# Attention products on block-diagonal matrices, or as 64x64 tiles of TensorE

## The chip, the cores and the metric

The kernel runs on one core of one Trainium2 chip. The core has five engines with an instruction queue each: TensorE (PE) for matmuls, VectorE (DVE), ScalarE (ACT) and GpSimd (POOL) for elementwise work, and SyncE (SP), which here issues nearly all DMAs. PE's weight loads have a row of their own in the profile (PEld). SBUF is the memory on the core with 128 partitions; PSUM takes the results of matmuls; DRAM is behind the DMAs. The metric is the device time of one execution in microseconds (us).

## What is computed

First, an attention with a state, by the delta rule: 4 batches times 8 heads, 768 steps, 48 numbers a head. Then a layer with a rational activation on the 3072 tokens.

```python
# attention: q, k, v of (4, 8, 768, 48), beta of (4, 8, 768)
k_n = k / (norm(k) + 1e-6)
for t in range(S):
    y[t]  = q[t] @ state                       # state: 48 x 48 for each head
    v_old = state^T k_n[t]
    state = state + beta[t] * outer(k_n[t], v[t] - v_old)
# layer: x = y as (3072, 384), w_in (384, 2048), w_out (2048, 384)
h = x @ w_in
g = (a0 + a1 h + a2 h^2 + a3 h^3) / (1 + |b0| |h| + |b1| h^2 + 1e-6)
out = g @ w_out
```

## The kernel before

**Tiling.** The sequence is cut into 12 chunks of 64 steps (`C`). In a chunk, the recurrence becomes small matrix products: for each of the 32 pairs of batch and head a 64x64 matrix of key products, the inverse of a triangular matrix made from it, and products with the state. Of the 32, two (of two batches, `b` = 0 and 1) are laid one above the other on the 128 partitions, so that 16 (`HP`, numbered `m`; two "pairs" `p` of eight heads `h`) lie side by side. Every operand is split in two f16 parts, and a product is three matmuls (`PASSES`: high times high, low times high, high times low).

**A product before** (`mm3`, `mm3p`, line 470) is 48 matmuls of the full array: two pairs, three passes, eight heads. For the two batches not to mix, the stationary matrix is block-diagonal, 128x128 with a 64x64 block for `b` = 0 and one for `b` = 1, and zeros elsewhere. `to_diagonal` (line 491) makes these matrices with DMAs on SyncE's queue, into buffers that are zeroed once (`SHAPE`, `diag`, line 197): `kbd` for the keys by feature (two buffers), `qbd` for the queries, `knbd` for the keys by time, `wbd` for the inverse `wc` and, before that, for the split key products `gl`, `ebd` for the off-diagonal blocks, and `mbd` for the masked query products. All but `kbd` have one buffer.

**Stages of a chunk.** `keys_normalized` splits the keys into `kn` (line 242, 248; one buffer for keys and queries alike), stores them to DRAM (`xdk`) and reads them back transposed (`tk`); the first chunk is transposed on PE. `key_products` forms `pg`, copies it negated to `g`, stores `g` in DRAM (`gd`) and splits it into `gl`. `inverse` reads 16x16 blocks of it (`gb`), inverts on DVE (lines 604 to 650), and brings the result over DRAM (`img`) to `wc`. `off_blocks` forms `pe` from `gl` and `wc`, and splits it into `et`, which goes to `ebd` in six DMAs (line 676); of each block column only what lies under the diagonal goes into `ebd`, by the choice of what is copied. `query_products` forms `pm` and masks it; `residual`, `solve_start`, three times `solve_step`, `solved`, `state_next` and `outputs` use these matrices on PE (`pk`, `pu`, `pd`, `py`). `tokens` transposes the output for the layer.

**The layer.** For each chunk there are eight units of 256 hidden features: `hidden` (18 matmuls, line 851), `numerator` and `quotient` (13 or so elementwise operations of 128x512, lines 868 to 898), and `accumulate` (12 matmuls, line 913).

**Order.** An opening works off the first chunks' attention and the conversion of the 64-bit weights (`ORDER`, line 1018). Then a loop over 96 units issues with each unit one eighth of the attention of later chunks (`attention`, line 1010: `back` of chunk c+1, `middle` of c+2, `front` of c+3, `ahead` of c+4). A scheduler that works at build time then sets the order on each engine from the priorities (`tc.high_priority`), and engines work strictly in that order. `BEHIND` (line 97) holds some loads until a named DMA is issued: those of chunk 1 behind `kbd` of chunk 0. The attention's front part shares one PSUM buffer (`ps_f`), the back part another (`ps_c`).

Of the kernel before, what the change touches and what calls it, by code (L numbers as in the profile page):

```python
# [10 lines left out]
F16 = mybir.dt.float16  # L11
# [27 lines left out]
def kernel(  # L39
# [16 lines left out]
    P = 128  # L56
# [15 lines left out]
    SHAPE = {  # L72
        "k": [P, NPAIR, 2, NH, 2, C, HG],
        "q": [P, NPAIR, 2, NH, 2, C, HG],
        "kn": [P, NPAIR, 2, H, 2, DP],
        "e": [P, 2, HP, 2, C],
        "w": [P, HP, 2, C, 2],
        "m": [P, 2, NG, 2, C, HG],
    }
# [17 lines left out]
    BEHIND = {"k1": "kbd0", "v1": "kbd0", "q1": "gb0", "k2": "gb0", "v2": "gb0", "q2": "gb0", "knbd0": "gb0"}  # L97
# [35 lines left out]
    )  # L133
    ones = cpool.tile([P, P], F32, name="ones")
# [66 lines left out]
    kn_b = zeroed(1, [P, 2, H, 2, DP], F16, "kn", lambda t: t[:, :, :, :, D:DP])[0]  # L201
    wt_b = zeroed(1, [P, 272], F32, "wt")
    diag = {
        nm: zeroed(
            2 if nm == "k" else 1,
            shape,
            F16,
            nm + "bd",
            eng=nc.vector if nm in "kwe" else nc.gpsimd,
        )  # L210
        for nm, shape in SHAPE.items()
    }
# [230 lines left out]
    def head(t, part, m):  # L443

        p, h = divmod(m, H)
        if t.shape[1] == HP:
            t = t[:, m, ..., part]
        elif t.shape[3] == NH and t.shape[-1] == HG:
            t = t[:, p, part, h // HG, ..., h % HG]
        elif t.shape[2] == HP:  # L450
            t = t[:, part, m]
        elif t.shape[3] == H:
            t = t[:, p, part, h]
        else:
            t = t[:, part, m // HG, ..., m % HG]
        return t.rearrange("p b x -> p (b x)") if len(t.shape) == 3 else t

    def alternating(t):

        return t.rearrange("p g x a -> p g a x")  # L460

    def mm3(dst, bd, rt, start=True, stop=True):

        for p in PAIRS:
            mm3p(dst, bd, rt, p, start, stop)

    def mm3p(dst, bd, rt, p, start=True, stop=True):
        for n, (lp, rp) in enumerate(PASSES):
            for h in range(H):
                nc.tensor.matmul(  # L470
                    dst[p][:, h],
                    head(bd, lp, p * H + h),
                    head(rt, rp, p * H + h),
                    start=start and n == 0 and h == 0,
                    stop=stop and n == len(PASSES) - 1,
                    skip_group_check=True,
                )

    def bank(pool, nm, w):

        t = pool.tile([P, NPAIR, 512], F32, tag="a", name=nm)[:, :, : H * w].rearrange("x p (h w) -> x p h w", w=w)
        return t[:, 0], t[:, 1], t
# [7 lines left out]

    def to_diagonal(nm, t, c=0):
        bd = diag[nm][c % len(diag[nm])]
        for b in range(2):
            sl = slice(b * C, (b + 1) * C)
            if nm == "kn":
                for a in range(HG):
                    nc.sync.dma_start(
                        out=bd[sl].rearrange("t p i (n a) b d -> t (p i n) a b d", a=HG)[:, :, a, b],
                        in_=t[:, :, :, :, a, b].rearrange("p i n t d -> t (p i n) d"),
                    )  # L500
            elif nm in "kq":
                dma = nc.sync.dma_start(
                    out=bd[sl, :, :, :, b].rearrange("x p i n t a -> x (p i n) (t a)"),
                    in_=t[sl].rearrange("x p i n t a -> x (p i n) (t a)"),
                )
                mark(nm + "bd", c, dma)
            elif nm == "w":
                nc.sync.dma_start(out=bd[sl, :, b, : t.shape[2]], in_=t[sl])
            else:
                nc.sync.dma_start(out=bd[sl, :, :, b, : t.shape[3]], in_=t[sl])  # L510
        return bd

    def grouped(t):

        return t.rearrange("p (g a) x -> p g a x", a=HG)

    def transposed(x, src, nm, soon):
# [8 lines left out]
        xd = dpool.tile([NPAIR, 2, NH, C, HG, 2, DP], F16, tag="xd" + nm[0], name=f"xd{nm}", bufs=4 if nm[0] == "k" else 2)  # L526
        for p in PAIRS:
            nc.sync.dma_start(
                out=xd[p].rearrange("i n t a b d -> t (i n) (a b d)"),
                in_=x[p * C : (p + 1) * C].rearrange("t i (n a) b d -> t (i n) (a b d)", n=NH),  # L530
            )
        t = sb.tile([P, NPAIR, 2, NH, C, HG], F16, tag="tt", name="t" + nm)
        if soon:
# [10 lines left out]
            return t, xd  # L544
# [5 lines left out]
        return t, xd  # L550
# [5 lines left out]
    def keys_normalized(c):  # L556
# [16 lines left out]
        t, kd = transposed(kn_b, kt, f"k_{c}", c == 0)  # L573
        info[c] = {"tk": t, "kd": kd}

    def keys_transposed(c):
        d = info[c]
        d["kbd"] = to_diagonal("k", d["tk"], c)

    def key_products(c):  # L580
        d = info[c]
        gd = d["gd"] = dpool.tile([P, BS], F32, tag="gd", name=f"gd_{c}")
        pg = bank(ps_f, f"pg_{c}", C)
        mm3(pg, d["kbd"], d.pop("tk"))
        g = sb.tile([P, HP, C], F32, tag="g", name=f"g_{c}", bufs=1)
        nc.scalar.mul(by_pair(g), pg[2], -1.0)
        for b in range(2):
            nc.sync.dma_start(out=as_rows(gd, b), in_=g[b * C : (b + 1) * C])
        gl = sb.tile([P, HP, C - 16, 2], F16, tag="gl", name=f"gl_{c}", bufs=1)
        split16([gl[..., i] for i in range(2)], g[:, :, : C - 16], eng=nc.gpsimd, hi=nc.gpsimd)  # L590
        d["gl"] = gl

    def inverse(c):
# [7 lines left out]
        wt = wt_b[0]  # L601
# [56 lines left out]
        wc = d["wc"] = sb.tile([P, HP, C, 2], F16, tag="wc", name=f"wc_{c}", bufs=1)  # L658
# [4 lines left out]
    def off_blocks(c):  # L663

        d = info[c]
        gbd, wc = d.pop("gbd"), d.pop("wc")
# [6 lines left out]
        for b in range(2):  # L673
# [30 lines left out]
    def queries_transposed(c):  # L704
        d = info[c]
        qt = d.pop("qt")
        scaled(qt, d["sq"])
        d["tq"] = transposed(kn_b, qt, f"q_{c}", c == 0)[0]

    def diagonals(c):  # L710
        d = info[c]
        if c > 0:
            d["qbd"] = to_diagonal("q", d.pop("tq"))
        d["mbd"] = to_diagonal("m", d.pop("mm"))
# [376 lines left out]
```

## Time and profile before

| | us |
|---|---|
| median of 3 runs | 855.29 |
| lowest, highest | 854.32, 863.12 |
| the profiled execution | 859.42 |
| its span, first to last instruction | 857.2 |
| busy PE (matmuls) | 622.0 |
| busy DVE | 760.8 |
| busy ACT | 544.9 |
| busy POOL | 482.7 |

The mean granted clock of TensorE over the span was 0.886 of full speed.

How to read it: a row of a group gives line, engine and operation, then output<-inputs by the program's names, shape and count, then busy time in us and mean ns of one, and then the engine's idle time ahead of them with what ended it. "L470 PE" are the attention's products. A row of waits gives who waited for whom: us in total, times, the longest. The chain of waits is the work that ended last, followed back from the end; "SPq" is time in the issue on SyncE's queue. Matmuls are pipelined, and their ends are modelled.

### The profile page before, as it was taken

Reading aid. Unit: us, or ns where it says so; the run is one execution under the profiler, and the core shown is the slowest. Engines: PE = TensorE matmul, PEld = TensorE weight load, DVE = VectorE, ACT = ScalarE, POOL = GpSimd, SP = SyncE. Lnnn points to the kernel's source line nnn. Section 1 sums busy time; section 2 is a strip of 40 time slices with the busy share of each in tenths; the row PEclk is TensorE's granted clock in tenths of the full one; section 3 lists DMA queues with packets and bytes.
Section 4 is the critical chain, followed back from the end, with each engine's and each line's share of the span. In section 5 each row is a group of like instructions: output and inputs, shape, how many; then the busy total and the mean of one; then the engine's idle time right before and its main releaser. Section 6 shows DMA issues by size and latency. Waiting matters only on the chain.

```text
span 857.2 us, 22995 instructions
## 1 busy us (share of the span) xinstructions
PE 622.0 (73%) x9290; PEld 492.0 (57%) x9290; DVE 760.8 (89%) x1312; ACT 544.9 (64%) x980; POOL 482.7 (56%) x452
## 2 busy tenths in 40 slices
PE   0220344766878688878798697995987989999895
PEld 0220344546666475666586585774775767777663
DVE  5998799697989969989989968999789999898996
ACT  4766656645666465677586574766566766677774
POOL 7655666355326437646736864766665635454532
PEclk9755555897988989989999899998989999999999
DMA  8996868898787875965997988598778672500000
GB/s 235 247 205 132 191 160 152 152 159 152 141 142 130 154 147 89 176 116 104 186 151 132 151 137 173 90 167 150 123 151 153 94 151 47 102 2 20 1 20 19
DMA packets 466506, 111.46 MB, mean 130 GB/s; under 512 B 431328, under 2 KB 463072, under 8 KB 466400
## 3 DMA queue, kind: packets, MB, share of 16 engines
q1 hardware_dynamic: 464224, 108.83, 67.8%
q8 instruction: 73, 1.20, 0.6%
q10 hardware_dynamic: 2176, 1.17, 0.5%
q14 instruction: 33, 0.27, 0.1%
HBM read 40.47 MB, written 26.23 MB: 78 GB/s over the span
## 4 chain that ended last, share of the span: by engine, by line
DVE 40%; DMA 16%; PE 14%; ACT 9%; issue 9%; SPq 7%; POOL 4%; POOLq 0%; ACTq 0%; DVEq 0%
PE ph L851 4%; PE po L913 4%; DVE mw L893 4%; DVE mw L873 3%; DVE mu L871 3%; DVE mg L892 3%; DVE mu L897 3%; DVE w_out L394 3%; DVE pr L636 2%; DVE mu L875 2%; DMA gd<-g 2%; DMA gb<-gd 2%; SPq L676 2%; POOL mg L898 2%; DMA wc<-img 1%
## 5 line engine op out<-in xcount | busy, mean ns | idle before, releaser
L913 PE MATMUL po<-w_out,mg 128*128 128x384 f16 x1152 | 224.9, 341 | 50.5 <-POOL mg L898 43.0
L851 PE MATMUL ph<-xT,w_in 128*128 128x256 f16 x1728 | 216.6, 278 | 13.1 <-DVE mu L875 11.4
L898 POOL TENSOR_TENSOR mg<-mu,mr 128x512 f16<-128x512 f32 x96 | 134.1, 1398 | 115.0 <-DVE mu L897 85.3
L851 PEld LDWEIGHTS <-w_in 128*128 128x128 f16 x1728 | 169.2, 100 | 45.5 <-issue 12.5
L913 PEld LDWEIGHTS <-mg 128*128 128x128 f16 x1152 | 110.2, 101 | 126.5 <-POOL mg L898 51.3
L868 ACT ACTIVATE mu<-ph,coef,msc 128x512 f32<-128x512 f32 x96 | 74.0, 771 | 45.5 <-POOL mg L898 31.0
L874 ACT ACTIVATE mw<-mw 128x512 f32<-128x512 f32 x96 | 60.3, 628 | 64.4 <-DVE mw L873 64.1
L893 DVE SCALAR_TENSOR_TENSOR mw<-mw,msc,mg 128x512 f32<-128x512 f32 x96 | 96.1, 1002 | 0.5
L470 PEld LDWEIGHTS <-kbd 128*128 128x128 f16 x1680 | 61.9, 105 | 36.4 <-issue 27.8
L871 DVE TENSOR_TENSOR mu<-ph,mu 128x512 f32<-128x512 f32 x96 | 65.4, 681 | 19.1 <-ACT mr L870 16.5
L875 DVE SCALAR_TENSOR_TENSOR mu<-mu,msc,ph 128x512 f32<-128x512 f32 x96 | 70.7, 736 | 0.0
L873 DVE SCALAR_TENSOR_TENSOR mw<-mr,msc,ph 128x512 f32<-128x512 f32 x96 | 70.5, 735 | 0.0
L886 ACT ACTIVATE mr<-mw,msc 128x512 f32<-128x512 f32 x96 | 69.2, 720 | 1.5
L895 POOL TENSOR_TENSOR mu<-mu,mw 128x512 f32<-128x512 f32 x36 | 48.7, 1353 | 32.8 <-DVE mw L893 29.1
L870 ACT ACTIVATE mr<-ph,msc 128x512 f32<-128x512 f32 x96 | 65.3, 680 | 0.0
L470 PE MATMUL pu<-z,ebd 128*128 128x48 f16 x1728 | 53.3, 187 | 15.7 <-DVE z L250 14.2
L470 PEld LDWEIGHTS <-ebd 128*128 128x128 f16 x1728 | 52.6, 99 | 19.5 <-issue 16.8
L887 ACT ACTIVATE mr<-mr 128x512 f32<-128x512 f32 x96 | 60.3, 628 | 1.4
L892 DVE SCALAR_TENSOR_TENSOR mg<-mu,msc,mr 128x512 f16<-128x512 f32 x60 | 56.9, 949 | 4.3 <-ACT mr L887 4.3
L879 POOL TENSOR_SCALAR mu<-mu,msc 128x512 f32<-128x512 f32 x36 | 34.2, 949 | 38.8 <-DVE mu L875 38.7
L897 DVE SCALAR_TENSOR_TENSOR mu<-mu,msc,mw 128x512 f32<-128x512 f32 x60 | 54.3, 907 | 0.4
L470 PEld LDWEIGHTS <-wbd 128*128 128x128 f16 x1152 | 35.1, 99 | 33.9 <-issue 30.4
(211 smaller groups left out, 1247.8 us busy)
## 6 DMA issues: line engine op xcount, KB each, us to landing
wsi<-in_moe_w_in_dram SPq DMA_DIRECT2D x24, 256.0 KB, 5.2
xdk<-kn SPq DMA_DIRECT2D x24, 256.0 KB, 3.9
kbd<-tk SPq DMA_DIRECT2D x24, 256.0 KB, 4.5
gd<-g SPq DMA_DIRECT2D x24, 256.0 KB, 4.3
wso<-in_moe_w_out_dram SPq DMA_DIRECT2D x32, 192.0 KB, 4.3
xdq<-kn SPq DMA_DIRECT2D x24, 256.0 KB, 4.3
mbd<-mm SPq DMA_DIRECT2D x24, 256.0 KB, 5.0
wc<-img SPq DMA_DIRECT2D x24, 256.0 KB, 5.1
```

Source lines behind the costliest of these rows:

```text
L470: nc.tensor.matmul(dst[p][:, h], head(bd, lp, p * H + h), head(rt, rp, p * H + h), start=start and n == 0 and h == 0, stop=stop and n == l ...
L851: nc.tensor.matmul(ph[:, i], w_in[:, f2, wp, cc, i * P : (i + 1) * P], x[:, xp, cc], start=k == 0, stop=k == 3 * NCC - 1,)
L868: nc.scalar.activation(u, ph, AF.Identity, scale=A3, bias=a2)
L871: nc.vector.tensor_mul(u, ph, u)
L873: nc.vector.scalar_tensor_tensor(out=w, in0=z, scalar=B0, in1=ph, op0=ALU.add, op1=ALU.mult)
L875: nc.vector.scalar_tensor_tensor(out=u, in0=u, scalar=A1, in1=ph, op0=ALU.add, op1=ALU.mult)
L886: nc.scalar.activation(r, w, AF.Ln, bias=Q0)
L892: nc.vector.scalar_tensor_tensor(out=g[:, 0], in0=u, scalar=A0, in1=r, op0=ALU.add, op1=ALU.mult)
L893: nc.vector.scalar_tensor_tensor(out=w, in0=w, scalar=Q0, in1=g[:, 0], op0=ALU.add, op1=ALU.mult)
L897: nc.vector.scalar_tensor_tensor(out=u, in0=u, scalar=A0, in1=w, op0=ALU.add, op1=ALU.subtract)
L898: nc.gpsimd.tensor_mul(g[:, 1], u, r)
L913: nc.tensor.matmul(po[p], g[:, gp, i, p * P : (p + 1) * P], w_out[:, f2, wp, i], start=f2 == lo and i == 0 and k == 0, stop=f2 == hi - 1 a ...
```

## The change

The products no longer use block-diagonal matrices. `mm3` issues for each pair, pass and head two matmuls, one for each batch `b`, on partitions `b*64` to `b*64+63` of both operands and of the output: a 64x64 tile of PE each. That is 96 matmuls where 48 were. All `to_diagonal` copies, their buffers and their zeroing go.

So that the matrices can be used where they lie, some things are different. The keys have four buffers `kn`, and the queries a fifth. The keys by time of one half of the batches lie on the other half's partitions; `keys_moved` copies them to `kx` (two DMAs). The lower part under the diagonal, which the choice of copied blocks gave before, now comes from a second, masked copy of the key products (`gm`, three ACT operations with a scale of 0 or -1 a partition, `under`), which `gl` is split from. `gl` and `et` are two buffers each, with 16 zeroed columns; `wc` has two, `mm` and the transposed `tk` and `tq` three. The first chunk no longer stores its transposed operands in DRAM. Some loads now wait for the issue of `gd` in place of `kbd`. The scratch for software-issued DMAs is made smaller.

```diff
-    BEHIND = {"k1": "kbd0", "v1": "kbd0", "q1": "gb0", "k2": "gb0", "v2": "gb0", "q2": "gb0", "knbd0": "gb0"}
+    BEHIND = {"k1": "gd0", "v1": "gd0", "q1": "gb0", "k2": "gb0", "v2": "gb0", "q2": "gb0", "kx0": "gb0"}
...
+    under = cpool.tile([P, NB - 1], F32, name="under")
+    nc.vector.tensor_scalar_mul(under[:, 2:3], zmask[:, 3:4], -1.0)
+    for j in (1, 0):
+        nc.vector.tensor_sub(under[:, j : j + 1], under[:, j + 1 : j + 2], zmask[:, j + 1 : j + 2])
...
-    kn_b = zeroed(1, [P, 2, H, 2, DP], F16, "kn", lambda t: t[:, :, :, :, D:DP])[0]
-    wt_b = zeroed(1, [P, 272], F32, "wt")
-    diag = {
...
+    KN_BUFS = 4
+    kn_b = zeroed(KN_BUFS + 1, [P, 2, H, 2, DP], F16, "kn", lambda t: t[:, :, :, :, D:DP])
+    wt_b = zeroed(1, [P, 272], F32, "wt")[0]
+    gl_b = zeroed(2, [P, 2, HP, C], F16, "gl", lambda t: t[:, :, :, C - 16 :])
+    et_b = zeroed(2, [P, 2, HP, C], F16, "et", lambda t: t[:, :, :, :16])
...
+    def part_of(t, i, m, b):
+
+        t = t[b * C : (b + 1) * C]
         p, h = divmod(m, H)
...
+        if len(t.shape) == 6:
+            return t[:, p, i, h // HG, :, h % HG]
+        return t[:, m, :, i] if t.shape[1] == HP else t[:, i, m]
+
+    def keys_by_time(d):
+        def get(t, i, m, b):
+            p, h = divmod(m, H)
+            return (d["kn"][:, i, h, b] if p == b else d["kx"][:, i, h])[b * C : (b + 1) * C]
+
+        return get
+
+    def mm3(dst, left, right, start=True, stop=True, of=part_of):
 
         for p in PAIRS:
...
+            for n, (lp, rp) in enumerate(PASSES):
+                for h in range(H):
+                    for b in range(2):
+                        nc.tensor.matmul(
+                            dst[b * C : (b + 1) * C, p, h],
+                            of(left, lp, p * H + h, b),
+                            part_of(right, rp, p * H + h, b),
+                            start=start and n == 0 and h == 0,
+                            stop=stop and n == len(PASSES) - 1,
+                            skip_group_check=True,
+                        )
...
-    def to_diagonal(nm, t, c=0):
...
+    def keys_moved(c):
+
+        d = info[c]
+        kx = d["kx"] = sb.tile([P, 2, H, DP], F16, tag="kx", name=f"kx_{c}", bufs=2)
+        with behind("kx", c):
+            for b in range(2):
+                nc.sync.dma_start(
+                    out=kx[b * C : (b + 1) * C].rearrange("t i h d -> t (i h) d"),
+                    in_=d["kn"][(1 - b) * C : (2 - b) * C, :, :, b].rearrange("t i h d -> t (i h) d"),
+                )
...
-        mm3(pg, d["kbd"], d.pop("tk"))
+        mm3(pg, d["tk"], d["tk"])
         g = sb.tile([P, HP, C], F32, tag="g", name=f"g_{c}", bufs=1)
-        nc.scalar.mul(by_pair(g), pg[2], -1.0)
+        nc.scalar.mul(by_pair(g), pg, -1.0)
+        gm = sb.tile([P, HP, C - 16], F32, tag="gm", name=f"gm_{c}", bufs=1)
+        for j in range(NB - 1):
+            cl = slice(16 * j, 16 * j + 16)
+            nc.scalar.activation(by_pair(gm)[..., cl], pg[..., cl], AF.Copy, scale=under[:, j : j + 1])
...
-        mm3(pe, gbd, wc[:, :, 16:])
-        d["wbd"] = to_diagonal("w", wc)
-        et = sb.tile([P, 2, HP, C - 16], F16, tag="u0", name=f"et_{c}", bufs=1)
-        split16(parts_by_pair(et), pe[2], 1.0 / 256.0)
-        ebd = d["ebd"] = diag["e"][0]
-        for b in range(2):
-            for j in range(NB - 1):
-                sl = slice(b * C + 16 * j, b * C + 16 * j + 16)
-                nc.sync.dma_start(out=ebd[sl, :, :, b, 16 * (j + 1) :], in_=et[sl, :, :, 16 * j :])
+        mm3(pe, d.pop("gl"), d["wc"][:, :, 16:])
+        et = d["et"] = et_b[c % 2]
+        split16([by_pair(et[:, i, :, 16:]) for i in range(2)], pe, 1.0 / 256.0)
...
-        mm3(pd, d["knbd"], d["z"])
+        mm3(pd, None, d["z"], of=keys_by_time(d))
...
-    nc = _bacc.Bacc("TRN2", target_bir_lowering=False, num_devices=1)
+    nc = _bacc.Bacc("TRN2", target_bir_lowering=False, num_devices=1, dynamic_dma_scratch_size=1024)
```

More of the change, by code (lines that the diff above doesn't have):

```diff
@@ L525, in transposed @@
         )
[L526 to L532, printed above, removed]
+        t = sb.tile([P, NPAIR, 2, NH, C, HG], F16, tag="t" + nm[0], name="t" + nm, bufs=3)
         if soon:
@@ L543, in transposed @@
                     )
-            return t, xd
+            return t
+        xd = dpool.tile([NPAIR, 2, NH, C, HG, 2, DP], F16, tag="xd" + nm[0], name=f"xd{nm}")
+        for p in PAIRS:
+            nc.sync.dma_start(
+                out=xd[p].rearrange("i n t a b d -> t (i n) (a b d)"),
+                in_=x[p * C : (p + 1) * C].rearrange("t i (n a) b d -> t (i n) (a b d)", n=NH),
+            )
         nc.sync.dma_start(
@@ L583, in key_products @@
         pg = bank(ps_f, f"pg_{c}", C)
-        mm3(pg, d["kbd"], d.pop("tk"))
+        mm3(pg, d["tk"], d["tk"])
         g = sb.tile([P, HP, C], F32, tag="g", name=f"g_{c}", bufs=1)
-        nc.scalar.mul(by_pair(g), pg[2], -1.0)
+        nc.scalar.mul(by_pair(g), pg, -1.0)
[3 more added lines that the diff above has]
+            nc.scalar.activation(by_pair(gm)[..., cl], pg[..., cl], AF.Copy, scale=under[:, j : j + 1])
         for b in range(2):
[L588 to L591, printed above, removed]
+            dma = nc.sync.dma_start(out=as_rows(gd, b), in_=g[b * C : (b + 1) * C])
+            mark("gd", c, dma)
+        gl = d["gl"] = gl_b[c % 2]
+        split16([gl[:, i, :, : C - 16] for i in range(2)], gm, eng=nc.gpsimd, hi=nc.gpsimd)
     def inverse(c):
@@ L707, in queries_transposed @@
         scaled(qt, d["sq"])
[L708 to L714, printed above, removed]
-        if c + 1 < NCH:
-            with behind("knbd", c):
-                d["knbd"] = to_diagonal("kn", d.pop("kd"))
+        d["tq"] = transposed(kn_b[KN_BUFS], qt, f"q_{c}", c == 0)
     def query_products(c):
@@ L722, in query_products @@
         pm = bank(ps_f, f"pm_{c}", C)
-        mm3(pm, d["kbd"], d["tq"])
+        mm3(pm, d["tk"], d["tq"])
         m32 = sb.tile([P, HP, C], F32, tag="g", name=f"m32_{c}", bufs=1)
         nc.vector.tensor_mul(
-            m32, pm[2].rearrange("x p h t -> x (p h) t"), mask.unsqueeze(1).broadcast_to([P, HP, C])
+            m32, pm.rearrange("x p h t -> x (p h) t"), mask.unsqueeze(1).broadcast_to([P, HP, C])
         )
-        mm = d["mm"] = sb.tile([P, 2, NG, C, HG], F16, tag="mm", name=f"mm_{c}", bufs=1)
-        split16([alternating(mm[:, i]) for i in range(2)], grouped(m32), eng=nc.gpsimd)
+        mm = d["mm"] = sb.tile([P, 2, HP, C], F16, tag="mm", name=f"mm_{c}", bufs=3)
+        split16(parts(mm), m32, eng=nc.gpsimd)
     ys = {}
@@ L744, in residual @@
             pk = bank(ps_c, f"pk_{c}", D)
[L745 removed]
+            mm3(pk, d["tk"], d["sh"])
             nc.vector.scalar_tensor_tensor(
[L747 removed]
+                out=by_pair(rf), in0=by_pair(rf), scalar=d["sv"], in1=pk, op0=ALU.mult, op1=ALU.subtract
             )
@@ L760, in solve_step @@
         z = sb.tile([P, 2, HP, D], F16, tag="z", name=f"z_{c}_{it}", bufs=2)
-        split16(parts_by_pair(z), d["pu"][2], zmask[:, it : it + 1])
-        mm3(d["pu"], d["ebd"], z, start=False)
+        split16(parts_by_pair(z), d["pu"], zmask[:, it : it + 1])
+        mm3(d["pu"], d["et"], z, start=False)
     def solved(c):
@@ L784, in outputs @@
         if c > 0:
-            mm3(py, d["qbd"], d["sh"], stop=False)
-        mm3(py, d["mbd"], d["z"], start=c == 0)
+            mm3(py, d["tq"], d["sh"], stop=False)
+        mm3(py, d["mm"], d["z"], start=c == 0)
         y = ys[c] = sb.tile([P, NPAIR, DM], F32, tag="ob", name=f"y_{c}", bufs=1)
-        nc.scalar.activation(y.rearrange("x p (h d) -> x p h d", h=H), py[2], AF.Copy, scale=d["iy"])
+        nc.scalar.activation(y.rearrange("x p (h d) -> x p h d", h=H), py, AF.Copy, scale=d["iy"])
     toks = {}
```

106 lines of the change are left out of this document (16 added, 90 removed).

## The prediction

> **What bounds the kernel now.** I read the page first, then busy time by stage, then the chain of waits, then the groups and waits that the edit touches. The page's first two parts (busy time of each engine; tenths of 40 slices):
>
> ```profile
> span 857.2 us, 22995 instructions
> PE 622.0 (73%) x9290; PEld 492.0 (57%) x9290; DVE 760.8 (89%) x1312; ACT 544.9 (64%) x980; POOL 482.7 (56%) x452
> ...
> DVE  5998799697989969989989968999789999898996
> ...
> DMA  8996868898787875965997988598778672500000
> ```
>
> VectorE (DVE) is busy 89% of the span, almost evenly; the DMA engines are near full until the last quarter. The same by stage, first for everything, then for the attention's products alone (all of them have the helper's line, L470):
>
> ```profile
> 10.00:140.00 130.00, 36.83 (x596) 32.23 (x596) 114.42 (x330) 82.03 (x213) 81.10 (x111) 0.62 0.85 199
> 140.00:740.00 600.00, 484.05 (x7666) 384.88 (x7667) 538.25 (x835) 379.74 (x635) 343.03 (x278) 0.92 0.77 136
> ```
> ```profile
> 140.00:740.00 600.00, 163.76 (x5320) 161.11 (x5321) 0.92 0.77 136
> ```
>
> The columns are start:end, length, then busy time of PE, PEld, DVE, ACT and POOL (in the second table PE and PEld), granted clock, DMA share, GB/s. In the 600 us from 140 to 740, where attention and the expert layer run together, DVE works 538 and TensorE (PE) 484, of which 164 are the attention's products. So DVE is the bound, it idles 62 us there and 16 us between 10 and 140, and PE stands 54 us behind it. These 78 us of idling are the most that shorter waits can give back; DVE's own work hardly changes.
>
> The chain of work that ended last, by engine:
>
> ```profile
> DVE 40%; DMA 16%; PE 14%; ACT 9%; issue 9%; SPq 7%; POOL 4%; POOLq 0%; ACTq 0%; DVEq 0%
> ```
>
> DVE is only 40% of it: the chain often leaves DVE for a DMA (137 us) or the issue of one on SyncE's queue (SPq, 60 us).
>
> **What the change takes away: the copies.** The DMA issues (count, KB each, median us to landing):
>
> ```profile
> kbd<-tk SPq DMA_DIRECT2D x24, 256.0 KB, 4.5
> gd<-g SPq DMA_DIRECT2D x24, 256.0 KB, 4.3
> mbd<-mm SPq DMA_DIRECT2D x24, 256.0 KB, 5.0
> wbd<-wc SPq DMA_DIRECT2D x24, 256.0 KB, 4.6
> knbd<-xdk SPq DMA_DIRECT2D x44, 128.0 KB, 4.1
> qbd<-tq SPq DMA_DIRECT2D x22, 256.0 KB, 4.5
> wbd<-gl SPq DMA_DIRECT2D x24, 192.0 KB, 4.0
> ebd<-et SPq DMA_DIRECT2D x24, 48.0 KB, 3.0
> ebd<-et SPq DMA_DIRECT2D x24, 32.0 KB, 2.7
> ebd<-et SPq DMA_DIRECT2D x24, 16.0 KB, 2.3
> ```
>
> All rows but gd go: 234 issues. Their KB sum to 6144 (kbd) + 6144 + 6144 + 5632 + 5632 + 4608 + 2304 = 36.6 MB of the page's 111. In come 22 copies kx<-kn of 128 KB (64 partitions x 16 x 64 x 2 bytes), 2.8 MB; the first chunk also loses its four stores of keys and queries to DRAM, whose one reader was knbd. On the chain itself stand three of these transfers, and 45 pieces of their issue (L676, L497, L508, L510, L502); here are the transfers, and of the pieces the first and the last:
>
> ```profile
> 97.55 3.01 DMA ebd<-et
> 248.92 3.75 DMA kbd<-tk
> 632.20 3.89 DMA wbd<-wc
> ```
> ```profile
> 151.31 0.03 SPq L510
> ...
> 676.26 0.68 SPq L497
> ```
>
> The transfers make 10.7 us. The 45 pieces sum to 31.5 us, most of it the six small issues a chunk of L676 (24 pieces, 17.0 us). Together 42 us. They are not all gain: DVE's total stays, and where a copy leaves, another operand is late next: after kbd goes the products wait for the transpose tk, after wbd for wc, after ebd for DVE's half of the split. What speaks for a good part is that these issues also block the queue behind them. Waits of SyncE's queue and of GpSimd (POOL) that fall away:
>
> ```profile
> SPq L508 <- PE pe L470: 17.1, 4, 8.5
> SPq L502 <- DMA tk<-xdk: 9.8, 6, 3.1
> SPq L497 <- PE pd L470: 6.6, 2, 5.5
> ```
> ```profile
> POOL kn L242 <- DMA xdq<-kn: 23.0, 7, 5.2
> ```
>
> The copy of wc waited 17.1 us for the products pe to release wbd, with every later load behind it; keys have four buffers of their own in place of the one that they shared with the queries, so POOL no longer waits 23.0 us in seven places for the last store of kn. Bounds of the gain: 0 (all idle time comes back elsewhere) and 42 us. I take 27, nearer the upper end, because the released queue is a gain that the 42 doesn't count. For the kept transfers (137 less 10.7 = 126 us on the chain) I take 5% shorter, 6 us, since a third of the bytes leaves a DMA share of 0.77: bounds 0 and, in proportion to the bytes, 38 us.
>
> At the start DVE loses four memsets and POOL three, and POOL gains eight small ones:
>
> ```profile
> L197 DVE MEMSET kbd<- 128x2048 f32 x2 | 3.5, 1765 | 1.7 <-PEq L1077 1.3 <-issue 0.4
> L197 POOL MEMSET kn<- x1: 312/312/312, 2.5 to 2.5; 128x256 f32 x1
> 18.39 0.47 DVE L387 TENSOR_SCALAR w_out<-wai 128x256 uint32<-128x256 uint32 x1 [4.72 <-POOL wai L386]
> ```
>
> DVE's 7 us lie ahead of 18.39, where it waits 4.72 us for POOL anyway; POOL saves 3 x 1.8 - 8 x 0.31 = 2.9 us of which I count 1. No cover is lost there. The smaller scratch for software-issued DMAs concerns no queue of this page: nothing.
>
> **What it adds.** On ScalarE (ACT), three masked copies of 128x256 from PSUM a chunk, 36 in all. Nearest row:
>
> ```profile
> L411 ACT ACTIVATE w_in<-pfw 128x256 bf16<-128x256 f32 x8 | 3.0, 380 | 1.6 <-DVE sw L409 1.6
> ```
>
> 36 x 0.38 = 13.7 us, 1.1 us a chunk. Behind them in ACT's queue stand the expert layer's activations, and the PSUM buffer of the key products (one buffer, whose next user is the sum of squares) comes free 1.1 us later. ACT is busy 380 of 600, so most is hidden: between 0 and 13.7 us; I take 2, about ACT's 9% of the chain and a little. The store of g, which the inverse reads, needs g alone, and g is made before the masked copies, so the inverse doesn't start later for them. The new wait, kx for its buffer of two chunks before and for kn, is met long ahead; behind it on SyncE's queue stand the loads, and it is 2 issues where knbd had 4.
>
> **The products themselves** decide the sign. Their 6192 matmuls become 12,384, two 64x64 tiles for each block-diagonal matrix. PE's timeline of now, 48 matmuls in a group:
>
> ```profile
> 496.32 1.37 PE L470 MATMUL pd<-z,knbd 128*128 128x48 f16 x48
> 498.62 1.60 PE L470 MATMUL pg<-tk,kbd 128*128 128x64 f16 x48
> ```
> ```profile
> L470 PE MATMUL pu<-z,ebd x1728: 182/183/248, 107.1 to 772.1; 128*128 128x48 f16 x192
> L470 PE MATMUL pg<-tk,kbd x576: 190/193/261, 27.9 to 675.7; 128*128 128x64 f16 x192
> ```
>
> Each takes 183 to 193 ns from start to end, but they follow each other every (1370 - 183) / 47 = 25 ns at 48 columns, and every (1600 - 193) / 47 = 30 ns at 64, weight load included. No trace shows two tiles. The lower bound for a pair of tiles is 25 ns (they run beside each other, on different rows and columns of the array), the next 50 (one after the other). On the chain the products have 30 pieces with 40.6 us, the first and the last:
>
> ```profile
> 91.03 2.09 PE pe L470 x48
> ...
> 759.61 1.22 PE pu L470 x48
> ```
>
> So each ns more for a pair costs 40.6 / 25 = 1.6 us. Beside each other they need a load or a matmul issued every 6 to 7 ns, where the rows show one every 12.5. I take 27 ns all the same, near the lower bound, since the two tiles share neither rows nor columns nor PSUM partitions, and since the step moves with the columns (30 against 25), which speaks for the array and not the issue as the limit: +3 us, with 0 and +41 as ends. And PE changes its shape at each border between these groups and the 128x128 work. With 6192 / 48 = 129 groups that is at most 258 borders. Bounds for one are 0 and what hides of a matmul's length now, 183 - 25 = 158 ns, in all 41 us of PE, of which a fifth is on the chain (PE has 14% of it, and is busy 73% of the span): 0 to 8 us. I take 4.
>
> The Trainium skill, TensorEngine Tiling (Array Packing), Key Properties, says that changing the tiling mode drains the array. By it the upper end would hold, 8 us in place of 4, and the sum would be 4 us longer; no run here shows it yet.
>
> Sum: -27 - 6 - 1 + 2 + 3 + 4 = **-25 us**. The profiled execution took 859.4 us (span 857.2 and 2.2 around it), so it would take 834; the median of the runs shown is 855.3, 4 lower, so 830. Ends for this case: with 42 + 12 of gain and no cost about 803, with 12 of gain and 8 of cost about 847.
>
> **The rivals.** *One tile after the other.* Place: PE between 140 and 740. At 50 ns a pair the 164 us double, PE needs 484 + 164 = 648 us in a stretch of 600 and becomes the bound in DVE's place. At 100% busy that is +48 us, at DVE's present 90% +120; by the chain it is +41 - 34 + 2 + 4 = +13. On the median that gives 868 to 975; I take 895, between the chain's figure and that of a fully busy PE (903), for the chain counts no queueing and the stretch doesn't count what the opening wins. It decides from the point at which PE reaches DVE's 538 us, (164 + 54) / 164 x 25 = 33 ns a pair, and turns the chain's balance at 25 x (1 + 25 / 41) = 40 ns. For it: 25 ns may be a floor for each matmul whatever its tile, as the issue below 12.5 ns is not shown. Against it: the step that moves with the columns. Chance 0.27.
>
> *Weight loads that no longer hide.* Loads now, f16 and f32, 128 columns each:
>
> ```profile
> L470 PEld LDWEIGHTS <-ebd 128*128 128x128 f16 x1728 | 52.6, 99 | 19.5 <-issue 16.8 <-DMA ebd<-et 1.3
> L819 PEld LDWEIGHTS px<-identf,y 128*128 128x128 f32 x72 | 9.1, 154 | 3.4 <-ACT sf L812 2.6 <-ACT sf L815 0.4
> 495.51 0.74 PEld L819 LDWEIGHTS px<-identf,y 128*128 128x128 f32 x6
> ```
>
> If a load of 64 columns went at the f32 step, (740 - 154) / 5 = 117 ns for 128, a tile would take 59 ns. Even with two tiles beside each other the 164 us become 387, PE needs 707 of 600, and at 95% busy the time is about 1000; serially far more. The f32 step holds a slower matmul too, which speaks against taking it for the load. Chance 0.07. The same page of the Trainium skill, Feature Incompatibilities, says that column tiling excludes the fast weight load; it is the rule behind this rival, and no row of a 64-column load is here to test it.
>
> *The copies were hidden.* DVE is the bound, the tiles are neutral, and what leaves the chain comes back as DVE's own queue: 853 (848 to 858). For it: DVE at 90%. Against: 78 us of idle. Chance 0.16.
>
> **Numbers.** Forecast 0.50 (803 to 847), serial tiles 0.27, loads 0.07, hidden copies 0.16. The likeliest gives 830. The range 803 to 930 leaves out some 0.06 below, and above it the slow loads and a quarter of the serial case, about 0.2 in all. Over 1% (8.6 us, about what a measurement can tell here) faster: 0.48 + 0.05 + 0.01 = 0.54; within: 0.02 + 0.09 + 0.03 = 0.14; slower: 0.23 + 0.07 + 0.02 = 0.32.
>
> **What would show it.** Groups of 96 tile matmuls should last about 1.5 us as the 48 do now; 2.6 or more says serial. The PE row should stay near 622 us and DVE near 754, the DMA digits fall by about a third until 740, SPq on the chain drop from 7% to about 3%, and no kn row wait for its store. I am wrong if PE shows more than 538 us in the shared stretch, or if DVE's idle time stays at 78 with the copies gone.

## The result and the profile after

The changed kernel takes **1019.4 us** (median; 1017.6 to 1024.5) beside 855.4 us for the kernel before on the same chip: 1.190 times as long, with an interval of 1.182 to 1.199. The prediction said 830, with a range of 803 to 930.

From the page of the changed kernel, the span, busy time by engine, and tenths of 40 slices for DVE, TensorE's granted clock and the DMA engines:

```profile
span 1017.3 us, 35020 instructions
PE 771.6 (76%) x15482; PEld 583.8 (57%) x15482; DVE 737.4 (72%) x1311; ACT 558.5 (55%) x1016; POOL 451.8 (44%) x457
...
DVE  3999955877756876667678586676676676687896
...
PEclk9555557877878869878879878878879879999999
DMA  7869474595540561643442442433352230000000
```

DVE has 23 us less work than before and is busy 72% instead of 89%; the DMA digits fell by more than a third from the second quarter on. PE has grown by 150 us, but is not full either. By stage (start:end, length, busy time of PE, PEld, DVE, ACT and POOL, granted clock, DMA share, GB/s), then for the attention's products alone (PE and PEld):

```profile
10.00:140.00 130.00, 39.36 (x1026) 35.00 (x1026) 115.29 (x334) 80.53 (x220) 80.60 (x106) 0.58 0.73 162
140.00:740.00 600.00, 487.46 (x10220) 368.53 (x10220) 409.82 (x657) 309.62 (x528) 255.86 (x229) 0.81 0.45 77
```
```profile
140.00:740.00 600.00, 208.68 (x8435) 184.27 (x8435) 0.81 0.45 77
```

The opening is as it was. In the 600 us of the shared stretch DVE finishes 410 us of work where it finished 538, ACT 310 where it finished 380. PE works 487, which is 81%, and no engine is the bound. So the time went into waiting, all along the stretch. The chain of waits by engine, and the waits (who waited for whom: us in total, times, the longest):

```profile
DVE 25%; DMA 17%; PE 16%; issue 13%; ACT 12%; POOL 10%; SPq 6%; POOLq 0%; ACTq 0%; DVEq 0%
```
```profile
ACT mw L825 <- DVE mw L824: 156.2, 77, 7.6
...
ACT mu L819 <- PE ph L802: 78.8, 24, 10.6
...
PE pm L453 <- DMA tq<-xdq: 44.1, 11, 8.9
PE pu L453 <- DVE z L239: 43.5, 16, 5.7
DVE ab L582 <- DMA gb<-gd: 43.3, 10, 6.5
```

DVE fell from 40% to 25% of the chain. PE stands for the transposed queries (44 us) and for the split parts `z` in the steps of the solve (43.5), DVE for the blocks of `g` on their way over DRAM (43.3 us). Behind these waits, in the same engines' queues, stand the layer's instructions, and ACT and POOL then wait for the layer's own steps: ACT's wait for DVE in L825 has more than doubled. The rows of the kernel before:

```profile
ACT mw L874 <- DVE mw L873: 64.1, 50, 4.6
...
DVE ab L615 <- DMA gb<-gd: 4.1, 5, 2.1
```

The transfers waited for are not much slower, though (`gd` lands after a median of 4.2 us, 4.3 before; `tq` after 4.8, 4.6 before; `gb` after 3.2, 4.6 before). That points to steps that come too early in the queues for what they wait for.

The tiles themselves, from PE's timeline (start, duration, and the idle time ahead, if any); then a fence with the stretches of the third and the second of them, columns as by stage:

```profile
571.33 2.75 PE L453 MATMUL pu<-z,et 64*64 64x48 f16 x96 [5.56 <-DVE z L239]
...
599.87 1.71 PE L453 MATMUL py<-sh,tq 64*64 64x48 f16 x96
...
604.83 2.77 PE L453 MATMUL pm<-tq,tk 64*64 64x64 f16 x96 [3.00 <-DMA tq<-xdq]
...
615.08 1.70 PE L453 MATMUL pk<-sh,tk 64*64 64x48 f16 x96
```
```profile
604.90:607.50 2.60, 2.60 (x100) 2.60 (x102) 2.60 (x5) 0.63 (x1) 0.00 (x0) 0.50 0.56 141
599.90:601.50 1.60, 1.60 (x103) 1.60 (x104) 1.60 (x3) 1.57 (x4) 0.00 (x0) 1.00 0.48 89
```

With 0.19 us for the last one to end, a tile follows every (1.70 - 0.19) / 95 = 16 ns, a pair of tiles every **32 ns**; behind a wait, where the granted clock is 0.50, a pair takes 54. So the two tiles do run beside each other, at a price a little above the 27 ns of the prediction. That can't be 164 us: the products' 41 us on the chain would grow by 1.6 us for each ns.

What else is odd in the timeline is this:

```profile
579.95 0.28 PE L802 MATMUL ph<-xT,w_in 128*128 128x256 f16 x1
580.16 0.21 PE L453 MATMUL pd<-z,kn 64*64 64x48 f16 x1
580.30 0.28 PE L802 MATMUL ph<-xT,w_in 128*128 128x256 f16 x1
580.52 0.21 PE L453 MATMUL pd<-z,kx 64*64 64x48 f16 x1
...
597.81 2.13 PE L802 MATMUL ph<-xT,w_in 128*128 128x256 f16 x18
```

The order merges a tile product with a layer product, one matmul of each by turns. Such a couple takes 580.30 - 579.95 = 0.35 us where a layer matmul in a group of its own takes (2.13 - 0.28) / 17 = 0.109 and a tile 0.016: each change of shape costs about **0.11 us**. In PE's order there are 566 borders between tiles and full matmuls; the kernel before has 206 between its products and the rest. Since borders were 206 and are 566 now, the order of the instructions is not what it was.

### The profile page after: what moved, and what is told of

Its sections match the earlier page's. It is cut to its first block, busy times and chain, and to the rows that moved or that the text cites. A ratio compares the mean times of both kernels' runs of the same rounds, so it can differ in the third digit from the quotient of the medians.

```text
span 1017.3 us, 35020 instructions
## 1 busy us (share of the span) xinstructions
PE 771.6 (76%) x15482; PEld 583.8 (57%) x15482; DVE 737.4 (72%) x1311; ACT 558.5 (55%) x1016; POOL 451.8 (44%) x457
## 4 chain that ended last, share of the span: by engine, by line
DVE 25%; DMA 17%; PE 16%; issue 13%; ACT 12%; POOL 10%; SPq 6%; POOLq 0%; ACTq 0%; DVEq 0%
PE po L864 4%; PE ph L802 4%; DMA xdq<-kn 3%; DMA v<-in_v_dram 3%; DVE mw L844 3%; DVE mw L824 3%; DMA tq<-xdq 3%; DVE mu L822 3%; DVE w_out L383 2%; DMA gd<-g 2%; ACT mu L819 2%; SPq L113 2%; DMA q<-in_q_dram 2%; PE py L453 2%; PE pu L453 2%
## 5 line engine op out<-in xcount | busy, mean ns | idle before, releaser
L864 PE MATMUL po<-w_out,mg 128*128 128x384 f16 x1152 | 247.0, 351 | 13.7 <-POOL mg L849 13.0
L802 PE MATMUL ph<-xT,w_in 128*128 128x256 f16 x1728 | 248.8, 291 | 2.9 <-ACT mr L837 1.4
L849 POOL TENSOR_TENSOR mg<-mu,mr 128x512 f16<-128x512 f32 x96 | 127.9, 1332 | 166.9 <-DVE mu L848 144.8
L802 PEld LDWEIGHTS <-w_in 128*128 128x128 f16 x1728 | 174.4, 103 | 45.6 <-issue 6.4
L825 ACT ACTIVATE mw<-mw 128x512 f32<-128x512 f32 x96 | 60.6, 632 | 157.0 <-DVE mw L824 156.2
L453 PEld LDWEIGHTS <-tk 64*64 64x64 f16 x3360 | 77.2, 129 | 76.3 <-DMA tq<-xdq 41.5
L453 PE MATMUL pu<-z,et 64*64 64x48 f16 x3456 | 76.1, 197 | 47.2 <-DVE z L239 43.5
L453 PEld LDWEIGHTS <-et 64*64 64x64 f16 x3456 | 73.2, 121 | 56.7 <-issue 55.7
L844 DVE SCALAR_TENSOR_TENSOR mw<-mw,msc,mg 128x512 f32<-128x512 f32 x96 | 87.8, 914 | 1.6
L453 PE MATMUL pm<-tq,tk 64*64 64x64 f16 x1152 | 32.5, 231 | 46.8 <-DMA tq<-xdq 44.1
L843 DVE SCALAR_TENSOR_TENSOR mg<-mu,msc,mr 128x512 f16<-128x512 f32 x60 | 49.8, 830 | 18.6 <-ACT mr L838 18.6
```

What stands on the lines that cost most here:

```text
L453: nc.tensor.matmul(dst[b * C : (b + 1) * C, p, h], of(left, lp, p * H + h, b), part_of(right, rp, p * H + h, b), start=start and n == 0 an ...
L802: nc.tensor.matmul(ph[:, i], w_in[:, f2, wp, cc, i * P : (i + 1) * P], x[:, xp, cc], start=k == 0, stop=k == 3 * NCC - 1,)
L825: nc.scalar.activation(w, w, AF.Abs)
L844: nc.vector.scalar_tensor_tensor(out=w, in0=w, scalar=Q0, in1=g[:, 0], op0=ALU.add, op1=ALU.mult)
L849: nc.gpsimd.tensor_mul(g[:, 1], u, r)
L864: nc.tensor.matmul(po[p], g[:, gp, i, p * P : (p + 1) * P], w_out[:, f2, wp, i], start=f2 == lo and i == 0 and k == 0, stop=f2 == hi - 1 a ...
```

## Experiments

Four readings competed: the merged groups and their borders; the price of the tiles; the shorter lead that twice as many instructions leave to the attention's steps (`high_priority(300)` counts instructions); and a different plan, because the planner (the scheduler that fixes the order at build time) has a price for each instruction, and the products are other instructions now. Ratios are against the kernel before on the same chip. A run's time in us is its own chip's, so where two runs of different chips are subtracted, the ratios are a second reading.

### Merged groups, or the lead

The changed kernel with twice the lead, which leaves 200 borders:

```diff
-            with tc.high_priority(300):
+            with tc.high_priority(600):
...
-            with tc.high_priority(1000):
+            with tc.high_priority(2000):
```

> The changed kernel with one number different: every lead of 300 in the order's priorities is 600. Theory 'merged groups': a lead is counted in instructions, the change doubles the matmuls of the attention, so 300 no longer lifts a group clear of the layer's matmuls and the two are merged one by one; each border between 64x64 and 128x128 costs PE some 0.12 us, and state_next lasts 12 to 22 us where it took 1.2. With 600 the order has 200 borders where the changed kernel has 566 (before: 206); so state_next is back at about 1.5 us and the time at 830 to 880. Theory 'dear tiles': a pair of tiles (32 ns where one block-diagonal matmul took 25) and the shape's price at each group are the cause, wherever they stand: 990 or more.

Measured: **1001.8 us**, ratio 1.170 (1.164 to 1.175). PE lost 73 us of busy time (698.5), and the time fell by 18. The shared stretch:

```profile
140.00:740.00 600.00, 440.53 (x10385) 352.23 (x10386) 409.79 (x677) 313.18 (x540) 256.00 (x233) 0.86 0.44 77
```

DVE's work there is what it was in the changed kernel, 410 us. The theory of merged groups had 830 to 880 and is refuted. The borders are real, but go with only about a tenth of the loss.

The kernel before with half the lead, without tiles:

```diff
-            with tc.high_priority(300):
+            with tc.high_priority(150):
...
-            with tc.high_priority(1000):
+            with tc.high_priority(500):
```

> The kernel before with all leads halved (150 and 500), full-array matmuls on block diagonals: a lead that is as short, measured in groups, as the one of the changed kernel, but no change of shape on PE. 238 borders. 'Merged groups' with the shape's change as the price: 850 to 885. If the shorter lead itself, by a later order, were the cause: 950 or more.

Measured: 861.7 us, 1.006 (1.004 to 1.009). A short lead alone isn't the cause.

### The tiles alone

The kernel before with all its copies, whose products take the two diagonal blocks as two 64x64 tiles, with leads of 300 and of 600:

```diff
-                nc.tensor.matmul(
-                    dst[p][:, h],
-                    head(bd, lp, p * H + h),
-                    head(rt, rp, p * H + h),
...
+                for b in range(2):
+                    sl = slice(b * C, (b + 1) * C)
+                    nc.tensor.matmul(
+                        dst[p][sl, h],
+                        head(bd, lp, p * H + h)[sl, sl],
+                        head(rt, rp, p * H + h)[sl],
```

> The kernel before with all its copies to block diagonals, but each product as two 64x64 tiles on the two blocks of the diagonal; lead 300. Its order has 528 borders. 'Merged groups': 960 to 1040, as the changed kernel, though the copies are all there. 'Dear tiles': about 1000 too. If the loss came from what else the change does (buffers, the masked copy, the moved keys, the loads' new mark): about 860 to 880.

> The same with the leads doubled (600, and 2000 for 1000): 208 borders. 'Merged groups': 855 to 900, the tiles' own price alone (7 ns a pair and two changes of shape a group). 'Dear tiles': 990 or more. The difference to the changed kernel with lead 600 is what the copies cost: 5 to 40 us if they matter, nothing if they were hidden.

Measured: 1113.3 us, 1.300 (1.293 to 1.307), and 1069.8 us, 1.250 (1.243 to 1.256). The first is above what either theory had for it. So the tile matmuls alone bring the loss, and nothing else of the change is needed for it. The rest of the change, above all the copies that go, is a gain of 94 and 68 us in these orders. But 6192 pairs at 7 ns more are 43 us of PE, not 215 or 258. The tiles act through something else.

### The plan

The next kernel issues the same instructions as the changed one. Only the table that the planner reads while the kernel is built is altered: TensorE costs half its time a column, never goes to half clock, and a matmul counts at least 12.5 ns. The order that comes out has 252 borders. A second one has leads of 600 on top (210 borders).

```diff
+    import dataclasses as _dc
+    from concourse.hw_specs import TRN2Spec as _S
+    _S.PE_CLOCK = _dc.replace(_S.PE_CLOCK, entry_columns=100.0)
+    _S.PE_CYCLE = _S.PE_CYCLE / 2
+    _S.PE_CLOCK = _dc.replace(_S.PE_CLOCK, resting=_S.PE_CYCLE)
+    _S.PE_MIN_PASS_INTERVAL_NS = 12.5
     nc = _bacc.Bacc("TRN2", target_bir_lowering=False, num_devices=1, dynamic_dma_scratch_size=1024)
```

> The changed kernel, instruction for instruction, lead 300; only the scheduler, which fixes the order at build time, is told that PE's clock is twice as fast and never rests, and that a matmul needs 12.5 ns at least. Theory 'planned for a slow PE': the scheduler took each 64x64 matmul as dear as a full one, so it planned a chunk as longer than it is and put the steps that wait for memory too few layer units apart (3 units from the key products to the query products, where the order before had 6.4 and this one has 5); the engines, which keep the order, stand at those waits with no engine full. Then: 820 to 900, with 252 borders and DVE at 80% or more. Theory 'dear tiles': 980 or more, whatever the order.

> The same with leads of 600: 210 borders, state_next in one piece. 'Planned for a slow PE': 810 to 890, some 0 to 20 us below lead 300, as lead 600 took 18 from the changed kernel. 'Dear tiles': 970 or more.

Measured: **867.1 us**, 1.011 (1.006 to 1.016), and 867.4, 1.014 (1.010 to 1.018). The same work in another order takes 152 us less. The page's busy row and the shared stretch of the first:

```profile
PE 680.1 (79%) x15482; PEld 535.8 (62%) x15482; DVE 738.5 (86%) x1311; ACT 549.8 (64%) x1016; POOL 465.1 (54%) x457
```
```profile
140.00:740.00 600.00, 521.25 (x12445) 410.81 (x12444) 524.95 (x859) 387.16 (x680) 332.52 (x283) 0.93 0.49 84
```

The same 1311 instructions of DVE take the same 738 us, but 525 us of them now fit in the stretch where 410 us did, and the leads matter no longer.

The reverse: the kernel before, with its full matmuls and its copies, planned as if a matmul took at least 54 ns; and the kernel before planned with the cheap table of above.

```diff
...
+    from concourse.hw_specs import TRN2Spec as _S
+    _S.PE_MIN_PASS_INTERVAL_NS = 54.0
```

> The kernel before, instruction for instruction, with no tile in it; the scheduler is told that a matmul needs 54 ns at least. Its order now has the changed kernel's distances (query products 3 units after the key products). 'Planned for a slow PE': 930 to 1010, with engines idle as in the changed kernel. 'Dear tiles': 850 to 875, since nothing that runs is different.

> The kernel before, with the scheduler told of the fast PE of planned_cheap: how much of a gain there comes from the planning alone. 'Planned for a slow PE': within 3% of before (830 to 870), since PE is not what its plan turned on; query products 8 units after the key products. 'Dear tiles' says nothing of it.

Measured: **942.9 us**, 1.101 (1.098 to 1.105), and 885.9, 1.033 (1.029 to 1.037). Without a single tile the dear plan loses 86 us, about half of the changed kernel's 164, and shows the same waits. Its shared stretch and two of its waits:

```profile
140.00:740.00 600.00, 437.93 (x6599) 348.46 (x6600) 457.48 (x731) 333.23 (x557) 287.14 (x249) 0.86 0.70 126
```
```profile
ACT mw L874 <- DVE mw L873: 169.5, 72, 7.8
...
PE pm L470 <- DMA tq<-xdq: 36.4, 8, 7.4
```

Again no engine is full: PE 438, DVE 457 of 600. The cheap table missed its forecast for the kernel before (within 3%, 830 to 870): it costs 28 us there, so a low price is not by itself a good one. How far the plans differ shows in PE's order. One mark is how many layer units (18 matmuls `ph` each) stand between the key products `pg` and the query products `pm` of chunks 7 to 10:

```
kernel                          units from pg to pm     us
before                          5 to 7                  855
full_150                        5 to 7                  862
planned_cheap, _600             4 to 5                  867, 867
before_planned_cheap            7 to 8                  886
changed                         3                      1019
lead600                         3 to 4                 1002
tiles_on_copies_300, _600       3 to 4                 1113, 1070
before_planned_dear             3 to 4                  943
```

In the slow plans the query products, which wait for the transfer of `tq`, stand 3 to 4 units behind the key products, in the others 4 to 8. From the last matmul of `pg` to the first of `pm` it takes about as long in both, 30 to 31 us in before_planned_dear and 29 to 46 in the kernel before, so the slow plan gets fewer units done in that time. Engines take their queues strictly in order, so each such wait also holds the layer's work that stands behind it.

### What is left of the change in a good plan

Next a price between: 0.8 of the time a column and at least 16 ns, which makes a pair 37 to 48 ns for the planner, with leads of 300, 450 and 200; and the tiles on copies in the cheap plan.

```diff
...
+    _S.PE_CYCLE = _S.PE_CYCLE * 0.8
+    _S.PE_CLOCK = _dc.replace(_S.PE_CLOCK, entry_columns=100.0, resting=_S.PE_CYCLE)
+    _S.PE_MIN_PASS_INTERVAL_NS = 16.0
```

> The changed kernel, leads of 300, with only the planner's price for PE altered again: 0.8 of its own time per column at the full clock (never half clock), at least 16 ns a matmul. A pair of tiles then costs it 37 ns at 48 columns and 48 at 64, where the trace shows 32, and a layer matmul 0.8 of its own price in place of the 0.5 of the cheap plan. The order that comes out has 198 borders between tile groups and full matmuls (566 in the changed kernel, 252 in the cheap plan), and in the middle of the run five to seven layer units from pg to pm (three in the changed kernel, five in the cheap plan, six in the kernel before). Theory 'the price decides': a price nearer to the chip than the cheap one gives a plan no worse than it, 845 to 867 us, and if the fewer waits give the copies' gain back, below the kernel before's 855. Rival 'a pair of tiles leaves a remainder': PE's pairs at 32 ns in place of 25 and the borders cost as much as the copies were worth, so any good plan stays at 862 to 872.

> As planned_mid, with the leads at 450 and 1500: 190 borders, about the same distances between the steps of a chunk. Theory 'the price decides': within 8 us of planned_mid, 845 to 867. Rival 'a remainder': 862 to 872. If it differs from planned_mid by more than 10 us, small changes of the order are worth as much as what is left of the change, and a remainder of 1% can't be put down to the tiles.

> As planned_mid, with the leads at 200 and 666: 202 borders, about the same distances between the steps of a chunk. With planned_mid and planned_mid_450 it shows the spread that comes from details of the order alone. Theory 'the price decides': 845 to 867. Rival 'a remainder': 862 to 872.

> The kernel before with its copies to block diagonals, products as two 64x64 tiles on the diagonal blocks, in the cheap plan (as planned_cheap: PE at half its price, at least 12.5 ns a matmul); 324 borders. Against planned_cheap (867) it tells what taking the copies away is worth when the plan isn't the trouble. 'The copies were hidden': 867 to 875. The prediction's term for them (27 and 6 us): about 900. What the two earlier pairs of orders gave (68 and 94 us): 935 to 960. It has 72 borders more than planned_cheap, at 0.12 us at most 9 us, of which a part is on the path.

Measured: 856.7 us, 1.002 (0.999 to 1.004); 852.9, 0.997 (0.994 to 1.000); **850.8**, 0.996 (0.993 to 0.999). So 'the price decides' holds, and the remainder of 862 to 872 is refuted. Tiles on copies in the cheap plan: 915.0 us, 1.071 (1.067 to 1.076), which makes the copies, net of what replaces them, worth 915 - 867 = 48 us there. Beside before_planned_cheap the tiles cost 915 - 886 = 29. (The 915 is from another chip; by the ratios the two are 52 and 33.)

That left open why a good plan gains 5 us and not 25. The last three kernels take the mid table too: the kernel before with leads of 200 and of 300, and the tiles on copies with 200. Their edits are the lines shown above, put in these two kernels.

> The kernel before, planned like planned_mid_200 (PE at 0.8 of its price per column, at least 16 ns a matmul, leads of 200). If the change itself is worth its 20 to 25 us and only the kernel before's own plan fits it better: 870 to 876, as with the cheap plan (886 against 867). If the change is worth about nothing at equal plans: 848 to 856.

> The kernel before, planned like planned_mid (leads of 300), where the changed kernel took 856.7. Worth of the change at equal plans 20 to 25 us: 877 to 882. About nothing: 853 to 861. More than 10 us from before_planned_mid_200 would say that details of an order are as large as the difference in question.

> The kernel before with its copies, products as two 64x64 tiles on the diagonal blocks, planned like planned_mid_200; 224 borders. Against planned_mid_200 (851) it tells what the copies are worth with tiles; in the cheap plan it was 48 us, so about 899 if the copies' worth is 48 again, 884 for the prediction's 33, 851 to 858 if copies are hidden in a good plan. Against before_planned_mid_200 it tells the price of the tiles: 29 us in the cheap plan; the prediction's terms for pairs and borders are 7.

Measured: 858.3 us, 1.004 (1.001 to 1.006); **848.6**, 0.992 (0.988 to 0.995), the fastest of all here; and 897.6, 1.051 (1.045 to 1.056). The first two miss what was expected for a change worth nothing, 848 to 856 and 853 to 861, by 2 and 4 us, and are 12 and 28 us from what was expected for a gain of 20 to 25. In one plan table with leads of 200:

```
                      full matmuls      64x64 tiles
with copies           858.3             897.6    (+39)
without copies        not possible      850.8    (-47)
```

The change is worth 858.3 - 850.8 = 7.5 us at leads of 200 (6 by the ratios), and costs 856.7 - 848.6 = 8.1 us at 300: nothing, within what the detail of an order makes. The kernel before itself moved by 9.7 us between these leads, and the parts are four times that: -47 and +39. The shared stretch (all work, then the products alone) of the kernel before planned so, of tiles on its copies, and of the changed kernel, each with leads of 200:

```profile
140.00:740.00 600.00, 486.87 (x7807) 391.22 (x7807) 543.42 (x844) 385.31 (x645) 348.46 (x280) 0.95 0.78 139
...
140.00:740.00 600.00, 168.75 (x5417) 165.24 (x5417) 0.95 0.78 139
```
```profile
140.00:740.00 600.00, 506.97 (x12015) 401.93 (x12017) 520.47 (x799) 359.64 (x603) 329.47 (x269) 0.90 0.77 133
...
140.00:740.00 600.00, 192.16 (x9801) 181.45 (x9803) 0.90 0.77 133
```
```profile
10.00:140.00 130.00, 47.87 (x1355) 42.43 (x1355) 114.84 (x313) 80.72 (x206) 80.11 (x103) 0.62 0.82 174
140.00:740.00 600.00, 526.68 (x12930) 419.74 (x12931) 535.88 (x864) 396.47 (x688) 330.27 (x284) 0.95 0.51 86
...
140.00:740.00 600.00, 198.75 (x10528) 187.53 (x10528) 0.95 0.51 86
```

A pair costs PE 168.75 / 5417 = 31.2 ns as one full matmul, 192.16 / 4900 = 39.2 as two tiles on copies, and 198.75 / 5264 = 37.8 without copies, with whatever of borders and half clock counts as busy. For 6192 pairs that is 50 and 41 us more of PE. PE now stands 9 us behind DVE instead of 57, and leads the chain of waits. The kernel before planned so, then planned_mid_200:

```profile
DVE 33%; PE 19%; DMA 14%; issue 10%; ACT 9%; POOL 8%; SPq 6%; POOLq 0%; ACTq 0%; DVEq 0%
```
```profile
PE 31%; DVE 29%; DMA 14%; issue 8%; ACT 8%; POOL 6%; SPq 3%; POOLq 0%; ACTq 0%; DVEq 0%
```

This is where the copies' gain went: SyncE's issues fell from 6% of the chain to 3% and DVE from 33% to 29%, and PE rose from 19% to 31% (37% with tiles on copies). The 14% of the kernel before under its own plan are not the measure, for the mid table alone makes them 19%, and 26% at leads of 300.

## Why the prediction was wrong

**The step that failed** is one that the prediction doesn't contain. It summed the change's parts on the chain and the bounds of the kernel before, and so took for granted that each engine's order stays, with DVE as the bound. The order is made anew at each build, from a price for each instruction, and the change doubles the number of the products' matmuls that the planner has to price. What the trace had was the chip's price for a product; what the order needed was the planner's. With another price and nothing else the changed kernel went from 1019 to 867 or 857 (to 851 with leads of 200 besides), and the kernel before from 855 to 943. The section on the order names the scheduler; no term and no rival of the prediction does.

**The copies.** Predicted 27 us from the 42 on the chain, and 6 for the shorter kept transfers; measured 47 and 48 to 52 in the mid and the cheap plan, with tiles and net of the masked copies and moved keys. That is inside the ends of these terms, but they were undersized. What they are worth with full matmuls can't be tried, for these need the block diagonals.

**The tiles.** Concurrency was right: 32 ns a pair at full clock, 27 predicted, and *one tile after the other* at 50 is refuted. But the term of 3 us, and 4 for the shape changes, measured 39 us in the mid plan and 29 to 33 in the cheap one. The step counted only the products on the chain, 1.6 us for each ns, and by the same rule 8 ns would be 13 us. PE as a whole got 50 us more work, with half clock and borders, and 39 us of it arrived in the time. Its share of the chain was taken as fixed. In the mid plan at leads of 200 it went from 19% to 37% with tiles on copies, and the products' own pieces on it from 47 to 114 us. The prediction's own point at which PE becomes the bound, 33 ns a pair, is all but reached by 32, although its rival came there by another road.

**The rival of the slow weight load** may have had the right mechanism, but its size was wrong. Loads (shortest/median/longest in ns) of the kernel before and of planned_mid_200:

```profile
L470 PEld LDWEIGHTS <-ebd x1728: 95/96/292, 106.2 to 772.1; 128*128 128x128 f16 x192
```
```profile
L453 PEld LDWEIGHTS <-et x3456: 102/110/156, 79.3 to 767.0; 64*64 64x64 f16 x192
```

A load of 64 columns takes longer than one of 128 did. The step of a pair no longer moves with the output's columns (a group with 64 columns takes as long as one with 48), and it grows from 32 to 54 ns when the clock halves. Both would fit the load as the limit. A limit in the issue would fit them too, with four instructions a pair, one every 8 ns; no run measured loads or issue alone, so the cause of the 32 ns stays open. The Trainium skill, TensorEngine Tiling (Array Packing), Feature Incompatibilities, says that column tiling excludes the fast weight load; the longer loads, 110 against 96 ns, are in line with it. That a pair then costs 32 ns, and not the rival's 59, only the run shows.

**The border.** The upper end of 158 ns was near: 0.11 us. The same page of the Trainium skill, Key Properties, says that a change of tiling mode drains TensorE; the 0.11 us agree with it. The number of borders was not bounded by 258, since the order merges groups: it was 566. With 200 in lead600 the time was 18 us less, in an order that differs in other things as well.

**The copies were hidden** gave 853, and in the mid plans that is the time: 851 to 857. That is luck, for the reason it gave does not hold: tiles on copies are 47 us slower, and gain and loss cancel. DVE's idle time between 10 and 740 is the sign: 730 - 114.84 - 535.88 = 79 us in planned_mid_200, as the 78 before. By the prediction's last sentence it is wrong even there.

**Small steps.** The ends of the forecast's own case don't follow from its terms: 54 us of gain off 855 is 801, not 803, and 12 of gain with 8 of cost is 851, not 847. Neither bears on the outcome. The masked copies took a median of 0.48 us and not 0.38, 36 x 0.48 = 17 us of ACT. No kn row of POOL waits for its store any more, as said, and in the good plan SPq is 3% of the chain, as said; in the changed kernel it was 6%. The wait of the key copies (L538) for their buffer, which should be met long ahead, was not: 63.5 us on SyncE's queue, with the loads behind it. The stores of keys and queries (L497) stood there for their split even longer. The changed kernel, then planned_mid_200:

```profile
SPq L497 <- POOL kn L237: 169.5, 18, 21.8
...
SPq L538 <- PE pd L453: 63.5, 8, 15.5
```
```profile
SPq L497 <- POOL kn L237: 57.0, 11, 13.3
...
SPq L538 <- PE pm L453: 2.6, 1, 2.6
```

With another order these waits, too, are shorter.

**What stays open.** That the plan is the cause is shown both ways. Which of its moves costs how much is not: the distance of `pg` and `pm` sets the slow plans, with 3 to 4 units, apart from the others, and no kernel moved that one step alone. Among the others it does not go with the time: planned_mid_450 has 4 to 6 units and takes 853 us, before_planned_cheap 7 to 8 and takes 886. What price the planner had for a tile before it was altered no run shows.

## What to carry to other kernels

Where an order is planned at build time, a change of instructions is also a change of plan: compare the planner's price for the new instruction with the trace, and set the order of the two kernels side by side before any time is read as the worth of the change. When the time grows and no engine is full, look for steps that wait for transfers at the head of an in-order queue. Two quarter-array tiles in place of one block-diagonal matmul are no free trade: here the copies that they saved paid for them, and no more.

## What was not expected of the hardware

- Two 64x64 tiles on different rows and columns start almost together (within 0.01 us in these rows of the changed kernel), and the next pair 0.03 us later. A pair takes 32 ns at full clock, 54 at half.

```profile
578.82 0.19 PE L453 MATMUL pd<-z,kn 64*64 64x48 f16 x1
578.82 0.19 PE L453 MATMUL pd<-z,kx 64*64 64x48 f16 x1
578.85 0.19 PE L453 MATMUL pd<-z,kn 64*64 64x48 f16 x1
578.85 0.19 PE L453 MATMUL pd<-z,kx 64*64 64x48 f16 x1
```

- A change between 64x64 tiles and full matmuls costs about 0.11 us each way, in a matmul stream that otherwise steps by 16 and 109 ns.
- The mean granted clock was lower in the kernels whose TensorE waits more. Over all runs of each it was 0.81 to 0.85 of full speed in the changed kernel, 0.85 to 0.91 in before_planned_dear, 0.88 to 0.95 in the kernel before, and 0.88 to 0.96 in the changed kernel's mid plans. In the group behind a wait above it was 0.50. How much of the loss is the clock's no run separates.
